# The first head's first keys turned by TensorE, and a normalisation moved ahead of a fold in the last unit

## The chip, the cores and the metric

The kernel runs on one core of one Trainium2 chip. The metric is the device time in microseconds; the time before is the median of three runs. The profile is of one further execution of the same program.

## The reference, cut to what matters

The inputs are a prompt of 2048 tokens of width 512 (A_x), a cache of keys and values for 32 heads of 2048 positions and width 128, and weights. All are bfloat16.

```python
xn = layernorm(x)                                  # 2048 x 512
q = (xn @ wq)  as 32 heads of 128
p = softmax(q @ k_cache^T * 128 ** -0.5)           # 32 x 2048 x 2048
s = (p @ v_cache, heads side by side) @ wo         # 2048 x 512
# B: layernorm, w1, gelu, four shifts by 1 and 2 tokens, w2, residual,
#    layernorm, w3, gelu, w4, residual, on xn
g = silu(B(xn))
out = x + s * g
```

The change touches the attention alone: the keys of head 0 at the start, and the softmax sums and the normalisation of the last heads at the end.

## The kernel before, in words

The program is written in the order in which each engine is to work: `pin` keeps the written order of instructions on each engine and each queue. Pools of SBUF and PSUM buffers decide which later instruction has to wait for an earlier one to be done with a buffer.

**Units and slots.** The attention is cut into 128 units `(g, qt, hh)`: a group of four heads, a tile of 512 queries, and a head of the group. Each unit has 8 slots `p`; slot `n = 8u + p`. In a slot, `s_slot` (L211) makes the scores of two chunks of 128 keys against 512 queries, as `ps_s` with the keys on partitions, and ScalarE takes the exponential into `pT` (L222). Some slots later (`LAGS`, 4 to 12 slots), `pv_slot` (L240) multiplies the same chunk with the values into `ps_o`, of which there are two buffers. Between these matmuls stand the query projections (`q_mm`, L194), the output projection (`wo_mm`, L317) and the matmuls of the other branch (B).

**Keys.** `load_k(h, pieces)` (L168) brings quarters of 512 keys of head `h` from DRAM by a transposing DMA on SyncE's queue, so that `kT` has the 128 head dimensions on partitions. The values come plainly (`load_v`, L177).

**Softmax sums.** VectorE adds the exponentials of a unit (`add_first`, `add_next`, L225 to L233) and halves the sum twice (`fold`, L235, two additions, L237 and L238). For most units (`turned(u)`, units 4 to 125) a DMA turns the result and VectorE reduces it. For the others, `sums` (L251) does it with four matmuls of one column on TensorE, into `ps_sum`. The reciprocal goes to DRAM and comes back to all partitions as `rb` (L263, `bcast` L291). `norm` (L298) multiplies `ps_o` by `rb` into `oT` (L305 for the turned units), which also frees the `ps_o` buffer.

**The start** (L795 to L812). Two token tiles are loaded on SyncE's queue and two on ScalarE's. SyncE then issues the four key quarters of head 0, the values of head 0 and the keys and values of head 1. `warm_up(48)` (L467) has TensorE multiply the identity by itself 48 times. `first_stats` (L418) makes the layer norm of the four tiles on ScalarE, VectorE and GpSimd; ScalarE's last instruction in it is L442, the normalised tile 0. `first_tokens` (L472) has TensorE turn the four tiles (matmul with the identity), copies them back (`back`, L492 on ScalarE and L490 on VectorE), projects the queries in quarters (`q_part`), copies them (`q_back`, L505 and L503), and makes the first scores in halves of 256 queries (`s_half(k, i)`, L507), where `k` is the key quarter. Its written order is turn 0, 1, 3, project 0, turn 2, project 1 and 3, `s_half(0, 0)`, project 2, half of unit 1's query, `s_half(1, 0)`, and so on.

**The last units.** The main loop (L873) writes, for each slot, the scores first, then the values that are due, then the rest. At slot 0 of a unit it writes `add_next(u - 1, 3)` and, where unit `u - 1` is not turned, `fold(u - 1)` (L899 to L902). At slot 1 of units above `LATE` = 20 it writes `normed(u - 3)` (L909). `sums(u - 1)` follows at slot 4 in the last unit (L917). The only unit above `LATE` whose predecessor is not turned is the last, 127.

The functions that the change touches:

Of the kernel before, what the change touches and what calls it, by code (L numbers as in the profile page):

```python
# [8 lines left out]
ACT = mybir.ActivationFunctionType  # L9
ALU = mybir.AluOpType  # L10
FP32 = mybir.dt.float32
BF16 = mybir.dt.bfloat16
# [5 lines left out]
def kernel(  # L18
# [15 lines left out]
    nc = tc.nc  # L34
    P = nc.NUM_PARTITIONS
# [4 lines left out]
    _, H, Sk, Dh = A_k_cache.shape  # L40
# [15 lines left out]
    KSPLIT = 4  # L56
# [4 lines left out]
    WARM = 48  # L61
# [61 lines left out]
    def mm(out, lhsT, rhs, start, stop):  # L123
        mm_count[0] += out.shape[-1] / 512
        pin(nc.tensor.matmul(out=out, lhsT=lhsT, rhs=rhs, start=start, stop=stop))  # L125
# [42 lines left out]
    def load_k(h, pieces):  # L168
        w = Sk // KSPLIT
        for i in pieces:  # L170
            if i == 0:
                kTs[h] = kp.tile([P, Sk], BF16, name="kT")
            pin(nc.sync.dma_start(
                out=kTs[h][:, i * w:(i + 1) * w],
                in_=A_k_cache[0, h, i * w:(i + 1) * w, :], transpose=True))

    def load_v(h, halves, eng=nc.sync):  # L177
        v = A_v_cache[0, h].rearrange("(i p j) d -> p i j d", p=P, j=KJ)
# [56 lines left out]
    def fold(u):  # L235
        a = st[u]["acc"]
        pin(nc.vector.tensor_tensor(out=a[:, 0:2, :], in0=a[:, 0:2, :], in1=a[:, 2:4, :], op=ALU.add))  # L237
        pin(nc.vector.tensor_tensor(out=a[:, 0, :], in0=a[:, 0, :], in1=a[:, 1, :], op=ALU.add))  # L238
# [26 lines left out]
    def turned(u):  # L265
        return T0 <= u < T1
# [148 lines left out]
        pin(nc.vector.bn_aggr(out=mv1[t][:], in_=bn[:]))  # L415
        rsqrt(rs1[t][:], mv1[t][:, 1:2])

    def first_stats():  # L418
        junk = gtp.tile([P, D], BF16, tag="pre", name="pre")
        pin(nc.scalar.activation(  # L420
            out=junk[:], in_=ln[3][:], func=ACT.Identity, scale=1.0 / D, accum_out=mvA[:, 3, 0:1]))
        pin(nc.scalar.activation(
            out=junk[:], in_=ln[3][:], func=ACT.Square, scale=-1.0, bias=mvA[:, 3, 0:1],
            accum_out=mvA[:, 3, 1:2]))
        xn0 = ph1.tile([P, D], BF16, tag="xn", bufs=5, name="xn")
        nb = smp.tile([P, 1], FP32, tag="nm", name="nb")

        def power(t):
            pin(nc.gpsimd.tensor_tensor(
                out=rsA[:, t:t + 1], in0=mvA[:, t, 1:2], in1=nhalf[:, 0:1], op=ALU.pow))  # L430

        for t in range(3):
            pin(nc.vector.bn_stats(out=bnA[:, t, 0:2, :], in_=ln[t][:]))
            pin(nc.vector.bn_aggr(out=mvA[:, t, :], in_=bnA[:, t, :, :]))
            power(t)
            if t == 1:
                pin(nc.vector.tensor_scalar(
                    out=nb[:], in0=mvA[:, 0, 0:1], scalar1=rsA[:, 0:1], scalar2=-1.0, op0=ALU.mult, op1=ALU.mult))
                pin(nc.vector.tensor_scalar(
                    out=mvA[:, 3, 1:2], in0=mvA[:, 3, 1:2], scalar1=1.0 / D, scalar2=EPS, op0=ALU.mult, op1=ALU.add))  # L440
                power(3)
        pin(nc.scalar.activation(  # L442
            out=xn0[:], in_=ln.pop(0)[:], func=ACT.Identity, scale=rsA[:, 0:1], bias=nb[:]))
        xn1 = ln1_norm(1)
        xn3 = ln1_norm(3)
        return xn0, xn1, ln1_norm(2), xn3
# [6 lines left out]
    def ln1_norm(t):  # L453
        xin = ln.pop(t)
        xn = ph1.tile([P, D], BF16, tag="xn", bufs=5, name="xn")
        norm1(t, xn[:], xin[:])
        return xn
# [9 lines left out]
    def warm_up(n):  # L467
        wt = psS.tile([P, 2, 512], FP32, name="ps_s")
        for _ in range(n):
            mm(wt[:, 0, 0:P], ident[:], ident[:], True, True)  # L470
# [327 lines left out]
    pin(nc.scalar.activation(out=act1[:], in_=nhalf[:, 0:1], func=ACT.Identity))  # L798
    for h in range(HG - 1):
        load_w(h, nc.gpsimd)  # L800
    load_k(0, range(KSPLIT))
    load_v(0, (0, 1))
    for i in range(2):
        load_k(1, (2 * i, 2 * i + 1))
        load_v(1, (i,))
    warm_up(WARM)
    xns_0 = first_stats()
    load_w(HG - 1, nc.gpsimd)
    for t in range(4, 6):
        ln1_load(t, nc.gpsimd)  # L810
# [52 lines left out]
    def normed(u):  # L863
        norm(u)
        gg, qq, hh = units[u]
        if hh == HG - 1 and (gg, qq) in deferred:
            at((u + 4) * SPU + 4, lambda: pin(nc.sync.dma_start(out=o_d[(gg, qq)][:], in_=oTs[(gg, qq)][:])))
        elif hh == HG - 1:
            wo_todo.extend((gg, 4 * qq + ts) for ts in range(4))
            if gg == NG - 1:  # L870
                fin_load(4 * qq)

    for n in range(NS):  # L873
        u, p = divmod(n, SPU)
        mm_before = mm_count[0]
        if n >= HALF:
            s_slot(u, p)
        lag = next(v for lim, v in LAGS if n < lim)
        while pv_done <= n - lag:
            pv_slot(*divmod(pv_done, SPU))  # L880
            pv_done += 1
        if n in first_q:
            q_mm(*first_q[n])
        if n == 15:
            q_copy(3)
        if u == HG - 2 and p in (6, 7):
            q_mm(HG, (2 * p - 12, 2 * p - 11))
        if u == HG - 2 and p == 7:
            q_copy(HG)
        if u in (HG - 1, HG):  # L890
            if p < 2:
                q_mm(u + 2, (2 * p, 2 * p + 1))
            if p == 2:
                q_copy(u + 2)
        elif p in (0, 1) and HG < u < NU - 2:
            q_mm(u + 2, (2 * p, 2 * p + 1))
        if p == 0 and u >= 2 and turned(u - 2):
            turned_sums(u - 2)
        if p == 0 and u >= 1:  # L899
            add_next(u - 1, 3)  # L900
            if not turned(u - 1):
                fold(u - 1)  # L902
        if p == (1 if mlp.get("stage") == 2 or u >= QUIET else 2) and HG < u < NU - 2:
            q_copy(u + 2)
        if p == 2 and u >= 1 and turned(u - 1):
            fold(u - 1)
        if p == 3 and u >= 1 and turned(u - 1):
            acc_turn(u - 1)
        if p == 1 and u > LATE:  # L909
            normed(u - 3)  # L910
        if p == (3 if u >= LATE else 2) and u >= 2 and turned(u - 2):
            bcast(u - 2)
        if n in norms:
            normed(norms[n])
        if p == 2 and u > HG + 1 and not turned(u - 2):
            normed(u - 2)
        if p == (4 if u > T1 or u == T0 or u in (1, 2) else 3) and u >= 1 and not turned(u - 1):  # L917
            sums(u - 1)
        if p == (7 if u == 1 else 5 if u > T1 or u in (2, T0) else 4) and u >= 1 and not turned(u - 1):
            bcast(u - 1)  # L920
        if p in (3 if QUIET <= u < NU - 2 else 4, 5) and wo_todo:
            wo_mm(*wo_todo[0], (2, 3) if p == 5 else (0, 1), "xm" if u >= NU - 2 else "xa")
        if p in (1, 3) and u >= NU - 2:
            wo_held(*wo_todo[0], (0, 1) if p == 1 else (2, 3))
        if p == 6 and u >= QUIET:
            add_next(u, 2)
        if p == 6 and wo_box:
            gg, t = wo_todo.popleft()
            wo_post(gg, t)
            if gg == NG - 1:  # L930
                at(n + 5, lambda t=t: wo_out(t))
                if t % 4 < 3:
                    fin_load(t + 1)
        if p == 4:
            add_first(u)
        if p == 6 and u < QUIET:
            add_next(u, 2)
        if p in (2, 6):
            w = 2 * u + (p >= 4)
            want = -(-(w + 1 - W0) * NMM // (W1 - W0)) - done if w >= W0 else 0  # L940
            window = []
            if chunks and want > 0:
                left = chunks[0].size - mpos
                k = min(left, max(2, min(want, 4))) if chunks[0].size > DC else (4 if left == 4 and want >= 3 else 2)
                window = [k - k // 2, k // 2]
        if p in (2, 3, 6, 7) and window:
            for _ in range(window[p % 2]):
                if mpos == 0 and NCH - len(chunks) in hooks:
                    hooks.pop(NCH - len(chunks))(n)
                run = chunks[0]  # L950
                run(mpos, n)
                mpos += 1
                done += 1
                if mpos == run.size:
                    chunks.popleft()
                    mpos = 0
        for fn in todo.pop(n, ()):
            fn()
        x = mm_count[0] - mm_before - 4
        debt[0] = max(0.0, debt[0] + EXP_OVER - x) if n >= HALF else 0.0  # L960
        if act_late and debt[0] + SMALL <= ahead(n + 1) + ahead(n + 2):
            act_late.popleft()(n)
            debt[0] += SMALL
        if p == SPU - 1 and u >= 2 and turned(u - 2) and (u < LATE or u == NU - 1):
            normed(u - 2)
# [95 lines left out]
```

## Time and profile before

| what | before |
|---|---|
| median of three runs | 1247.88 us (1246.97 to 1249.35) |
| profiled execution, its own time | 1246.4 us |
| span of its instructions | 1244.6 us |
| instructions | 16527 |
| granted TensorE clock | 1.00 |
| transposing key loads (`kT`), issues | 128 |

The span runs from the first instruction to the end of the last one. A row of the timeline has start, length, engine, line, operation, output and inputs, count, and in brackets the idle time of the engine ahead of it with what ended it; lengths of several instructions are of the group. PE is the matmul, PEld the weight load of TensorE, and an engine's name with a q is its queue or sequencer. An idle time is put down to what came last by the profile. The chain of waits is followed back from the last instruction.

### The profile page before, as it was taken

Reading aid. Unit: us, or ns where it says so; the run is one execution under the profiler, and the core shown is the slowest. Engines: PE = TensorE matmul, PEld = TensorE weight load, DVE = VectorE, ACT = ScalarE, POOL = GpSimd, SP = SyncE. Lnnn points to the kernel's source line nnn. Section 1 sums busy time; section 2 is a strip of 40 time slices with the busy share of each in tenths; the row PEclk is TensorE's granted clock in tenths of the full one; section 3 lists DMA queues with packets and bytes.
Section 4 is the critical chain, followed back from the end, with each engine's and each line's share of the span. In section 5 each row is a group of like instructions: output and inputs, shape, how many; then the busy total and the mean of one; then the engine's idle time right before and its main releaser. Section 6 shows DMA issues by size and latency. Waiting matters only on the chain.

```text
span 1244.6 us, 16527 instructions
## 1 busy us (share of the span) xinstructions
PE 1232.4 (99%) x5702; PEld 597.3 (48%) x5816; DVE 1116.5 (90%) x1520; ACT 1129.0 (91%) x1285; POOL 172.2 (14%) x299
## 2 busy tenths in 40 slices
PE   9999999999999999999999999999999999999998
PEld 5444444444444444444444444444444444444444
DVE  7999999999899988899988889999888999888998
ACT  8999998888999888899998889998888999998992
POOL 5563003432111000000100000010000000000110
PEclk9999999999999999999999999999999999999999
DMA  9665573665634455234474235734446233563563
GB/s 202 124 118 101 101 141 77 129 126 123 145 65 112 100 102 120 55 89 75 109 148 90 68 77 111 132 76 82 86 101 124 56 89 65 127 140 76 105 149 108
DMA packets 248788, 131.42 MB, mean 106 GB/s; under 512 B 200000, under 2 KB 225472, under 8 KB 248704
## 3 DMA queue, kind: packets, MB, share of 16 engines
q1 hardware_dynamic: 239296, 104.46, 40.8%
q0 software_dynamic: 8832, 25.44, 9.3%
q8 instruction: 45, 0.74, 0.3%
q10 hardware_dynamic: 576, 0.46, 0.1%
q14 instruction: 39, 0.32, 0.1%
HBM read 83.62 MB, written 8.13 MB: 74 GB/s over the span
## 4 chain that ended last, share of the span: by engine, by line
PE 93%; DVE 3%; ACT 1%; DMA 1%; issue 1%; SPq 0%; DVEq 0%; ACTq 0%
PE ps_o L125 34%; PE ps_s L125 33%; PE ps_m L125 9%; PE ps_q L125 8%; PE ps_wo L125 8%; DVE acc L233 1%; ACT pT L222 1%; DMA kT<-in_A_k_cache_dram 1%; DVE oT L305 0%; DVE acc L228 0%; DMA rb<-dr 0%; DVE acc L237 0%; DVE sm L276 0%; DVE sq L554 0%; DVE s_acc L391 0%
## 5 line engine op out<-in xcount | busy, mean ns | idle before, releaser
L222 ACT ACTIVATE pT<-ps_s 128x1024 bf16<-128x1024 f32 x1020 | 1017.7, 1029 | 89.2 <-PE ps_s L125 72.9
L125 PE MATMUL ps_o<-pT,vb 128*128 128x512 bf16 x2027 | 602.9, 379 | 3.8 <-DVE oT L305 0.2
L125 PE MATMUL ps_s<-qT,kT 128*128 128x512 bf16 (+1 forms) x1992 | 595.3, 378 | 2.2 <-DMA kT<-in_A_k_cache_dram 0.7
L125 PEld LDWEIGHTS <-kT 128*128 128x128 bf16 x2056 | 232.4, 113 | 227.2 <-issue 2.4
L233 DVE TENSOR_TENSOR acc<-acc,pT 128x2048 bf16<-128x2048 bf16 x256 | 310.5, 1213 | 15.6 <-ACT pT L222 14.7
L125 PEld LDWEIGHTS <-vb 128*128 128x128 bf16 x2048 | 200.2, 98 | 225.8 <-issue 0.5
L228 DVE TENSOR_TENSOR acc<-pT 128x2048 bf16<-128x2048 bf16 x128 | 156.2, 1220 | 32.2 <-ACT pT L222 31.8
L125 PE MATMUL ps_q<-xnT,wq_h 128*128 128x512 bf16 (+1 forms) x517 | 151.3, 374 | 0.5
L125 PE MATMUL ps_wo<-wo_h,oT 128*128 128x512 bf16 (+1 forms) x453 | 133.8, 377 | 0.2
L305 DVE TENSOR_TENSOR oT<-ps_o,rb 128x512 bf16<-128x512 f32 x122 | 130.8, 1072 | 2.1 <-DMA rb<-dr 2.0
L391 DVE TENSOR_TENSOR s_acc<-ps_wo,s_acc 128x512 f32<-128x512 f32 x96 | 66.0, 687 | 41.2 <-PE ps_wo L125 40.5
L237 DVE TENSOR_TENSOR acc<-acc 128x1024 bf16<-128x1024 bf16 x128 | 87.4, 683 | 0.3
L276 DVE TENSOR_REDUCE sm<-accT 128x4 f32<-128x512 bf16 x122 | 82.8, 678 | 1.5 <-DMA accT<-acc 1.4
L125 PEld LDWEIGHTS <-wq_h 128*128 128x128 bf16 x524 | 50.7, 98 | 59.5 <-issue 0.8
L208 DVE CAST qT<-ps_q 128x512 bf16<-128x512 f32 x109 | 75.0, 688 | 3.1 <-PE ps_q L125 2.8
L125 PE MATMUL ps_m<-xn2T,w_sb 128*128 128x512 bf16 x218 | 75.3, 379 | 0.1
L125 PE MATMUL ps_m<-w_sb,h2T 128*128 128x512 bf16 x218 | 75.3, 379 | 0.1
L723 POOL DMA_DIRECT2D w_sb<-in_B_w_dram x28 | 21.1, 755 | 370.2 <-PE ps_m L125 328.4
L125 PEld LDWEIGHTS <-oT 128*128 128x128 bf16 x468 | 45.7, 98 | 54.5 <-DVE oT L312 0.5
L751 POOL DMA_DIRECT2D g_d<-xr x16 | 8.8, 548 | 438.3 <-DVE xr L749 438.3
L238 DVE TENSOR_TENSOR acc<-acc 128x512 bf16<-128x512 bf16 x128 | 54.4, 425 | 4.4
L554 DVE SCALAR_TENSOR_TENSOR sq<-sq,pre 128x1024 bf16<-128x1024 bf16 x36 | 44.0, 1222 | 4.6 <-ACT sq L550 4.5
(102 smaller groups left out, 633.5 us busy)
## 6 DMA issues: line engine op xcount, KB each, us to landing
rb<-dr SPq DMA_DIRECT2D x127, 256.0 KB, 3.8
vb<-in_A_v_cache_dram SPq DMA_DIRECT2D x62, 256.0 KB, 3.8
w_sb<-in_B_w_dram POOLq DMA_DIRECT2D x28, 256.0 KB, 4.6
wo_h<-in_A_wo_dram SPq DMA_DIRECT2D x32, 128.0 KB, 3.8
wq_h<-in_A_wq_dram SPq DMA_DIRECT2D x28, 128.0 KB, 3.5
kT<-in_A_k_cache_dram SPq DMA_TRANSPOSE x128, 3.8
dr<-rc SPq DMA_DIRECT2D x128, 2.0 KB, 2.4
xr<-in_A_x_dram POOLq DMA_DIRECT2D x16, 128.0 KB, 3.3
```

The source lines that it names most:

```text
L125: pin(nc.tensor.matmul(out=out, lhsT=lhsT, rhs=rhs, start=start, stop=stop))
L208: pin(nc.vector.tensor_copy(out=qT[:], in_=st[u].pop("psq")[:]))
L222: pin(nc.scalar.activation(out=s["pT"][-1][:, jj:jj + 2, :], in_=sps[:], func=ACT.Exp, scale=SCALE))
L228: pin(nc.vector.tensor_tensor(out=s["acc"][:], in0=s["pT"][0][:], in1=s["pT"][1][:], op=ALU.add))
L233: pin(nc.vector.tensor_tensor(out=a[:], in0=a[:], in1=st[u]["pT"][i][:], op=ALU.add))
L237: pin(nc.vector.tensor_tensor(out=a[:, 0:2, :], in0=a[:, 0:2, :], in1=a[:, 2:4, :], op=ALU.add))
L238: pin(nc.vector.tensor_tensor(out=a[:, 0, :], in0=a[:, 0, :], in1=a[:, 1, :], op=ALU.add))
L276: pin(nc.vector.tensor_reduce(out=sm[:], in_=s.pop("at")[:], axis=mybir.AxisListType.X, op=ALU.add))
L305: pin(nc.vector.tensor_tensor(out=oTs[(g, qt)][:, hh, :].rearrange(f, j=4), in0=s["o"].rearrange(f, j=4), in1=s["rb"].rearrange("x (p j) - ...
L391: pin(nc.vector.tensor_tensor(out=sa, in0=ps[:], in1=sa, op=ALU.add))
L554: pin(nc.vector.scalar_tensor_tensor(out=sq[:].rearrange(f2), in0=sq[:].rearrange(f2), scalar=1.0, in1=pre[:].rearrange(f2), op0=ALU.add, ...
L723: pin(nc.gpsimd.dma_start(out=w[:], in_=w3_v[:, :, fc * P:(fc + 2) * P]))
```

## The change

The first quarter of head 0's keys is no longer brought by a transposing DMA. `first_keys` loads it plainly, on the same queue and at the same place, into a tile `kn` with four consecutive keys on each partition (1 KB). `first_keys_turn` turns it on TensorE with four matmuls against the identity, into a PSUM buffer of the tag `xm`, in the place of four of the warm-up matmuls; four more warm-up matmuls follow it, so that there are 40, 4 and 4 where there were 48. `first_keys_back` copies it on ScalarE into the first quarter of `kT`, in the order that the transposing DMA gave, behind L442. `kn` takes a buffer of the tag `pre` ahead of the other users of that tag. The other three quarters of head 0, and all other heads, are loaded as before.

In the last unit, `fold(u - 1)` moves from slot 0 to slot 1, behind `normed(u - 3)`.

```diff
     def load_k(h, pieces):
         w = Sk // KSPLIT
         for i in pieces:
-            if i == 0:
+            if h not in kTs:
                 kTs[h] = kp.tile([P, Sk], BF16, name="kT")
...
+    def first_keys():
+        kTs[0] = kp.tile([P, Sk], BF16, name="kT")
+        kn = gtp.tile([P, KJ, Dh], BF16, tag="pre", name="kn")
+        pin(nc.sync.dma_start(
+            out=kn[:], in_=A_k_cache[0, 0, 0:Sk // KSPLIT, :].rearrange("(p j) d -> p j d", j=KJ)))
+        return kn
+
+    def first_keys_turn(kn):
+        tp = psX.tile([P, KJ, P], FP32, tag="xm", name="ps_k")
+        for j in range(KJ):
+            mm(tp[:, j, :], kn[:, j, :], ident[:], True, True)
+        return tp
+
+    def first_keys_back(tp):
+        pin(nc.scalar.activation(
+            out=kTs[0][:, 0:Sk // KSPLIT].rearrange("d (p j) -> d j p", j=KJ), in_=tp[:], func=ACT.Identity))
...
-    def first_stats():
+    def first_stats(behind):
...
             out=xn0[:], in_=ln.pop(0)[:], func=ACT.Identity, scale=rsA[:, 0:1], bias=nb[:]))
+        behind()
         xn1 = ln1_norm(1)
...
-    load_k(0, range(KSPLIT))
+    kn_0 = first_keys()
+    load_k(0, range(1, KSPLIT))
     load_v(0, (0, 1))
...
-    warm_up(WARM)
-    xns_0 = first_stats()
+    warm_up(WARM - 8)
+    tp_0 = first_keys_turn(kn_0)
+    warm_up(4)
+    xns_0 = first_stats(lambda: first_keys_back(tp_0))
...
             add_next(u - 1, 3)
-            if not turned(u - 1):
+            if not turned(u - 1) and u <= LATE:
                 fold(u - 1)
...
         if p == 1 and u > LATE:
             normed(u - 3)
+            if not turned(u - 1):
+                fold(u - 1)
```

## The prediction

> **What bounds the kernel now.** I read the page first, then TensorE's waits over the whole run, then the chain of waits, and then the timeline at the two places that the change touches.
>
> ```profile
> span 1244.6 us, 16527 instructions
> PE 1232.4 (99%) x5702; PEld 597.3 (48%) x5816; DVE 1116.5 (90%) x1520; ACT 1129.0 (91%) x1285; POOL 172.2 (14%) x299
> PE 93%; DVE 3%; ACT 1%; DMA 1%; issue 1%; SPq 0%; DVEq 0%; ACTq 0%
> ```
>
> TensorE (PE) is busy for 99% of the span, and 93% of the chain that ends last is its work. A gain can only come from time in which TensorE stands. The waits of TensorE in the whole run are three groups:
>
> ```profile
> PE ps_s L125 <- DVE ident L87: 1.4, 1, 1.4
> PE ps_s L125 <- DMA kT<-in_A_k_cache_dram: 0.7, 2, 0.5
> PE ps_o L125 <- DVE oT L305: 0.2, 1, 0.2
> ```
>
> The first is the start before the identity exists, and the change leaves it. The second is two waits for the first head's keys, the third one wait for a normalisation. The change goes at exactly these two. The chain at the start, in order of time (start, length, what):
>
> ```profile
> 1.65 1.23 SPq L173
> 2.92 7.28 DMA kT<-in_A_k_cache_dram
> 10.25 0.63 PE ps_s L125 x4
> 10.88 0.43 PE ps_q L125 x2
> ```
>
> So the run hangs on the second quarter of the keys: its transposing DMA is issued behind the first one on SyncE's queue, lands 7.28 us later at 10.20, and TensorE goes on at 10.25. From there TensorE has no recorded wait until the last normalisation at 1217: what the stream gains before 10.25 is kept to the end unless a new wait eats it.
>
> **Part 1, the first keys.** The rows of the start (start, length, engine, line, operation, count):
>
> ```profile
> 0.73 0.87 SPq L408 DMA_DIRECT2D xin<-in_A_x_dram  x2
> 1.39 4.74 PE L125 MATMUL ps_s<-ident 128*128 128x128 bf16 x48 [1.39 <-DVE ident L87]
> 1.65 5.13 SPq L173 DMA_TRANSPOSE kT<-in_A_k_cache_dram  x4
> 5.18 0.81 ACT L442 ACTIVATE xn<-xin,nb,rsA 128x512 bf16<-128x512 bf16 x1
> 6.48 1.08 ACT L492 ACTIVATE xnT<-ps_o 128x512 bf16<-128x512 f32 x2 [0.49 <-PE ps_o L125]
> 8.04 0.38 ACT L505 ACTIVATE qT<-ps_q 128x256 bf16<-128x256 f32 x1
> 9.01 0.63 PE L125 MATMUL ps_s<-qT,kT 128*128 128x256 bf16 x4 [0.52 <-DMA kT<-in_A_k_cache_dram]
> 9.47 0.60 PE L125 MATMUL ps_q<-xnT,wq_h 128*128 128x128 bf16 x5
> 10.25 0.63 PE L125 MATMUL ps_s<-qT,kT 128*128 128x256 bf16 x4 [0.18 <-DMA kT<-in_A_k_cache_dram]
> ```
>
> And the DMAs issued in the first 15 us (median us from issue to landing is last):
>
> ```profile
> vb<-in_A_v_cache_dram SPq DMA_DIRECT2D x4, 256.0 KB, 5.3
> wq_h<-in_A_wq_dram POOLq DMA_DIRECT2D x4, 128.0 KB, 5.7
> xin<-in_A_x_dram SPq DMA_DIRECT2D x2, 128.0 KB, 2.7
> kT<-in_A_k_cache_dram SPq DMA_TRANSPOSE x9, 6.4
> ```
>
> *SyncE's queue.* One of four transposing issues (5.13 / 4 = 1.28 us) becomes a plain one of the same 128 KB (0.87 / 2 = 0.44). Whatever stands behind it on SyncE is issued 0.84 us sooner: the second quarter of the keys at 2.10 in place of 2.92, then the third and fourth, the values and the next head's keys.
>
> *The plain keys, kn.* Issued at 1.65 behind the two x loads. The nearest row is that of those loads (same size, form and queue): 2.7 us, so 4.35. Bounds: not below 2.7, since it queues behind them; above, the value loads' 5.3 (6.95) and, at worst, the landing of the transposing load whose place it takes (8.95, just ahead of the matmul at 9.01 that waits for it). I take 4.5 to 5.0.
>
> *TensorE.* Forty of the 48 warm-up matmuls stay ahead of the turn. By the row's mean (4.74 / 48 = 0.1 us) the turn would stand at 5.3, an estimate that I give 0.3 us either way. Four matmuls that turn the keys and four that warm take the place of the last eight of the same form: no work is added, and nothing waits if kn has landed by about 5.3. If it has not, the token turns queued behind it wait too, and with them ScalarE.
>
> *ScalarE.* One new 128x512 copy out of PSUM stands between L442 (ends 5.99) and the first L492 (6.48). Two L492 in a row take 1.08, so 0.54 each; the hole is 0.49, which L492 spent waiting for TensorE. Cost on the path: 0.05 us. Its output is written with a stride of four elements, which no row of this kernel's ScalarE shows; bounds: nothing (a copy of that size out of PSUM is 0.54) and a doubling (another 0.54). I take nothing, because the L492 rows already read and write in pieces and cost no more than their size.
>
> *First scores.* They wait at 9.01 for kT. Without it they wait for the query copy L505, which ends at 8.42 and then, with 0.05 for the new copy and 0.05 for the signal, they start at 8.52: 0.49 sooner. The work between the first and the second score group (four matmuls of 256 columns, four of 128, two of 512) takes 10.25 - 9.01 - 0.18 = 1.06 by its rows, less if a record of the 9.47 group is missing, then up to 1.12. So the second group can start at 8.52 + 1.1 = 9.62, if its keys are there.
>
> *Second quarter of the keys.* It now has the place that the first had: issued at 2.10 in place of 1.65. The first landed 8.95 - 1.65 = 7.3 us after issue; the same gives 9.4, before 9.62. Bounds: 8.95 if landing is set by the other transfers and not by the issue, and 10.2 as now if it gains nothing. **Front: 10.25 - 9.62 = 0.63 us gained**, between 0.05 (landing at 10.2) and 0.7.
>
> [...]
>
> **Part 2, the normalisation.** It changes one unit, the last: two fold additions and one normalisation swap places on VectorE. Rows of VectorE and TensorE there:
>
> ```profile
> 1207.10 1.07 DVE L305 TENSOR_TENSOR oT<-ps_o,rb 128x512 bf16<-128x512 f32 x1
> 1208.09 0.68 DVE L237 TENSOR_TENSOR acc<-acc 128x1024 bf16<-128x1024 bf16 x1
> 1208.81 0.42 DVE L238 TENSOR_TENSOR acc<-acc 128x512 bf16<-128x512 bf16 x1
> 1215.31 0.69 DVE L237 TENSOR_TENSOR acc<-acc 128x1024 bf16<-128x1024 bf16 x1
> 1216.04 0.43 DVE L238 TENSOR_TENSOR acc<-acc 128x512 bf16<-128x512 bf16 x1
> 1216.38 1.07 DVE L305 TENSOR_TENSOR oT<-ps_o,rb 128x512 bf16<-128x512 f32 x1
> 1216.70 0.59 PE L125 MATMUL ps_s<-qT,kT 128*128 128x512 bf16 x2
> 1217.50 0.59 PE L125 MATMUL ps_o<-pT,vb 128*128 128x512 bf16 x2 [0.21 <-DVE oT L305]
> 1217.93 0.27 PE L125 MATMUL ps_sum<-ones_t,acc 128*128 128x1 bf16 x4
> 1225.37 0.21 PEld L125 LDWEIGHTS <-acc 128*128 128x128 bf16 x4 [0.30 <-DVE acc L238]
> ```
>
> The two score matmuls at 1216.70 would be followed 0.43 us later, as pairs are (10.88 in the chain), at 1217.13; the value matmuls start at 1217.50, when the normalisation has freed their PSUM buffer: 0.37 lost. In the new order it starts at 1215.31, where the fold did, and ends at 1216.38, before the value matmuls want the buffer at 1217.13; that wait goes. Its row from DRAM is needed 1.07 us sooner:
>
> ```profile
> L295 SPq DMA_DIRECT2D rb<-dr x2: 327/387/447, 1210.6 to 1217.5; - x2
> DMA to landing us min/median/max: 3.5/3.5/3.5
> ```
>
> Issued at 1210.6, landed at 1214.1: there in time. What is late next is the fold, which the sums read. From the triple at 1207.10, normalisation and both folds take 1208.81 + 0.42 - 1207.10 = 2.13, so the folds end at 1217.44, the sums want them at 1217.93 - 0.37 = 1217.56, with a weight load just ahead; the one at 1225.37 started 0.06 after its fold, so here 1217.50. Queued behind on TensorE is everything else, so a late fold costs one for one: I take 0.07, bounds 0 and 0.2. **Tail: 0.30 us gained**, between 0.17 and 0.37. VectorE's work behind the pair starts when it did (same three durations), and after 1217.5 the end follows TensorE.
>
> **Sum.** 0.63 + 0.30 = 0.93 us off the profiled execution: 1246.4 becomes 1245.5 (span 1244.6 to 1243.7). The profiled execution lies 1.5 under the median of the three runs, 1247.88, and those reach from 1246.97 to 1249.35. Off the median: **1247.0 us**, 0.07% faster. About 0.2% (2.5 us) is what a measurement of this kernel can tell from no change, so this is a forecast of no difference that shows.
>
> **Rivals.**
>
> *The second quarter lands no sooner* (about 10.2). For it: its landing lies among those of wq_h (5.7 us) and may be set by them. Against: it then has one transposing load fewer ahead. Front 0.05, total -0.35: 1247.5.
>
> *The tokens of the second query tile eat the gain.* Their last transposing load and the first matmul that reads it:
>
> ```profile
> L465 SPq DMA_TRANSPOSE xnT<-xn x1: 1283/1283/1283, 26.8 to 26.8; - x1
> DMA to landing us min/median/max: 3.8/3.8/3.8
> ...
> 30.66 0.59 PE L125 MATMUL ps_q<-xnT,wq_h 128*128 128x512 bf16 x2
> ```
>
> 26.8 + 3.8 = 30.6, and TensorE reads it at 30.66: no slack at all. If TensorE comes 0.63 sooner and this load does not, 0.6 is given back: total -0.3, 1247.6. Against it: SyncE's queue, on which it stands, is 0.84 sooner at the start.
>
> *Slower: kn lands late.* The turn stands in TensorE's order ahead of every token turn. kn must land by about 5.4 (four matmuls, then the copy of 0.54, before 6.48). Later it delays the first scores one for one; the front's gain is gone at 6.0, the tail's at 6.35. At the value loads' 5.3 us (6.95) the total is +0.6: 1248.5. At 8.95 it is +2.6: 1250.5. For it: most loads around it take 5 to 6 us. Against: the two ahead of it in its queue take 2.7.
>
> *The swap does nothing* (fold and sums late by as much as the normalisation is early): total -0.6, 1247.3.
>
> **How the numbers follow.** Forecast 0.60; second quarter no sooner 0.13; tokens 0.12; kn late 0.08; swap without effect 0.07. All but the extreme of the slow rival stay within 2.5 us of the present time. What reaches over the bound is mostly the spread of the runs (2.4 us between three of them): from -0.9 it takes 1.6 more to be faster by over 0.2%, chance 0.09, and 3.4 to be slower, which with the extreme of kn gives 0.05; within 0.2% 0.86. The range takes the same gain off the profiled execution and the highest run: 1246.4 - 0.9 = 1245.5 and 1249.35 - 0.9 = 1248.5, which holds all cases but the extreme one.
>
> **What would show it.** TensorE's waits for kT from DMA gone or under 0.1, and none for kn; first scores near 8.5, second near 9.6; SyncE's third entry 0.44 long; the first token matmul still near 6.05; the matmul at 30.66 near 30.0 without a wait; the value matmuls of the last unit 0.43 behind the scores. A first token matmul after 6.3 shows kn late; a second score group after 10.0 shows the second quarter unmoved; a wait of the sums for L238 over 0.2 us shows the swap empty. A time outside 1245.5 to 1248.5 with none of these waits in the trace would come from a mechanism that I have not named.

## The result, and the profile after

| | before | after |
|---|---|---|
| median (lowest to highest), 14 runs each | 1247.10 us (1246.58 to 1249.35) | 1249.74 us (1246.80 to 1252.02) |
| profiled execution, its span | 1246.4, 1244.6 us | 1248.48, 1246.7 us |

The ratio after to before is 1.0017 (95% interval 1.0010 to 1.0024): the change costs 2.6 us between the medians and 2.1 by the ratio. The ratio on record is not the quotient of the two medians, here as in the table below. A later measurement of the same two kernels, on one chip, gave 1.0015 (1.0006 to 1.0024), 1248.07 against 1246.49. The forecast was 0.9 us less, range 1245.5 to 1248.5; the time is above the range. The runs of after also spread over 5.2 us, those of before over 2.8; in the later measurement they spread over 2.8 and 3.0.

TensorE's waits in the whole run of after (engine, tile, line, releaser; us in total, times, longest):

```profile
PE ps_s L125 <- DVE ident L87: 1.4, 1, 1.4
PE ps_k L125 <- DMA kn<-in_A_k_cache_dram: 1.3, 1, 1.3
PE ps_q L125 <- issue: 0.5, 1, 0.5
PE ps_s L125 <- ACT qT L523: 0.2, 1, 0.2
```

The waits that the change aimed at, two for kT and one for the normalisation, are gone. A wait for kn stands in their place, and one without a named releaser. The chain of waits at the start of after (start, length, what):

```profile
1.65 5.44 DMA kn<-in_A_k_cache_dram
7.13 0.62 PE ps_k L125 x4
7.78 1.31 ACT kT L191
9.09 0.43 ACT xnT L510
...
11.18 0.60 PE ps_s L125 x4
11.78 0.44 PE ps_q L125 x5
...
12.27 0.60 PE ps_s L125 x4
```

Before, the run hung on the second quarter of the keys up to 10.25. Now it hangs on the new plain load, then on the new copy. The second score group starts at 12.27 in place of 10.25, **2.02 us later**. The timeline of after at that place:

```profile
1.39 4.45 PE L125 MATMUL ps_s<-ident 128*128 128x128 bf16 x40 [1.39 <-DVE ident L87]
1.65 0.42 SPq L180 DMA_DIRECT2D kn<-in_A_k_cache_dram  x1
2.12 3.81 SPq L173 DMA_TRANSPOSE kT<-in_A_k_cache_dram  x3
...
7.13 0.61 PE L125 MATMUL ps_k<-ident,kn 128*128 128x128 bf16 x4 [1.30 <-DMA kn<-in_A_k_cache_dram]
7.54 0.63 PE L125 MATMUL ps_s<-ident 128*128 128x128 bf16 x4
...
7.96 1.06 PE L125 MATMUL ps_o<-ident,xn 128*128 128x128 bf16 x8
```

The forty warm-up matmuls end at 5.84, and TensorE, whose order is pinned, stands 1.30 us, to 7.13, for kn, which lands at 7.09; the first token matmul goes from 6.05 to 7.96. The next place is the second query tile. The last two transposing loads of its tokens in after, and TensorE's row that reads the last one:

```profile
L483 SPq DMA_TRANSPOSE xnT<-xn x2: 1201/1209/1217, 25.7 to 27.0; - x2
DMA to landing us min/median/max: 5.2/5.7/6.2
```

```profile
32.19 0.59 PE L125 MATMUL ps_o<-pT,vb 128*128 128x512 bf16 x2
33.31 0.59 PE L125 MATMUL ps_q<-xnT,wq_h 128*128 128x512 bf16 x2 [0.53 <-issue]
```

The load issued at 27.0 takes 6.2 us (3.8 before) and lands at 33.2. The matmul behind it starts 1.12 after its neighbour in place of 0.43: **0.69 us lost**. And the last unit, from the timeline of after:

```profile
1217.45 1.07 DVE L322 TENSOR_TENSOR oT<-ps_o,rb 128x512 bf16<-128x512 f32 x1
1218.44 0.68 DVE L254 TENSOR_TENSOR acc<-acc 128x1024 bf16<-128x1024 bf16 x1
1219.15 0.42 DVE L255 TENSOR_TENSOR acc<-acc 128x512 bf16<-128x512 bf16 x1
1219.17 0.59 PE L125 MATMUL ps_s<-qT,kT 128*128 128x512 bf16 x2
1219.60 0.59 PE L125 MATMUL ps_o<-pT,vb 128*128 128x512 bf16 x2
1220.04 0.28 PE L125 MATMUL ps_sum<-ones_t,acc 128*128 128x1 bf16 x4
```

The normalisation stands ahead of both folds; the value matmuls follow the scores by 0.43 where it was 0.80, and the sums at 1220.04 find the fold done at 1219.57: **0.37 us gained**. Together +2.02 + 0.69 - 0.37 = +2.34; the spans differ by 2.1. The last unit's scores come 2.47 later than before (1219.17 against 1216.70), so the missing 0.24 was made up between the second tile and the last unit; where is not shown.

### The profile page after: what moved, and what is told of

Same layout as the page of the kernel before. It is cut to its first block, busy times and chain, and to the rows that moved or that the text cites. A ratio compares the mean times of both kernels' runs of the same rounds, so it can differ in the third digit from the quotient of the medians.

```text
span 1246.7 us, 16529 instructions
## 1 busy us (share of the span) xinstructions
PE 1233.3 (99%) x5702; PEld 598.9 (48%) x5816; DVE 1116.0 (90%) x1520; ACT 1130.1 (91%) x1286; POOL 173.1 (14%) x299
## 4 chain that ended last, share of the span: by engine, by line
PE 97%; ACT 1%; DVE 1%; issue 1%; DMA 0%; SPq 0%; ACTq 0%
PE ps_o L125 36%; PE ps_s L125 35%; PE ps_m L125 10%; PE ps_q L125 9%; PE ps_wo L125 8%; ACT pT L239 1%; DMA kn<-in_A_k_cache_dram 0%; DVE acc L250 0%; ACT kT L191 0%; DVE sq L572 0%; DVE oT L322 0%; SPq L425 0%; ACT pre L609 0%; PE ps_sum L125 0%; PE ps_k L125 0%
```

## The experiments

Four questions: is the tail's gain real; why does kn land late; what do the wait and the copy each cost; why do the second tile's tokens come late. Kernels in neighbouring rows with the same time of before ran on one chip and share those runs. A letter for a theory belongs to its own expectation; the words beside it count. "kn" below is the time from its issue (at 1.65 unless the edit moves it) to its landing.

| run | median us (runs) | before, same chip | ratio, 95% interval | kn, us |
|---|---|---|---|---|
| e1 swap only | 1246.42 (11) | 1246.97 | 0.9997, 0.9988 to 1.0005 | none |
| e2 keys only | 1248.69 (11) | 1246.97 | 1.0013, 1.0004 to 1.0022 | 5.1 |
| e3 dense copy | 1247.09 (11) | 1246.97 | 1.0001, 0.9992 to 1.0010 | 4.6 |
| e4 turns behind | 1247.46 (11) | 1246.97 | 1.0005, 0.9996 to 1.0013 | 4.6 |
| e5 wq behind | 1252.76 (1) | 1246.77 | none | 3.4 |
| e6 two wq behind | 1250.45 (6) | 1246.77 | 1.0031, 1.0019 to 1.0042 | 4.1 |
| e7 tokens behind | 1247.85 (11) | 1246.77 | 1.0007, 0.9998 to 1.0016 | 6.2 |
| e8 both | 1249.64 (9) | 1246.77 | 1.0024, 1.0014 to 1.0033 | 4.2 |
| e9 wq after norm | 1248.34 (11) | 1247.12 | 1.0009, 1.0000 to 1.0018 | 4.2 |
| e10 swap, tokens | 1246.76 (11) | 1247.12 | 0.9998, 0.9990 to 1.0007 | none |
| e11 late turn, tokens | 1246.88 (11) | 1247.12 | 0.9999, 0.9990 to 1.0008 | 5.1 |
| e12 late turn, wq | 1248.91 (11) | 1247.12 | 1.0018, 1.0009 to 1.0027 | 4.2 |
| e13 late turn | 1247.10 (11) | 1246.49 | 1.0006, 0.9997 to 1.0015 | 6.2 |
| e14 after again | 1248.07 (11) | 1246.49 | 1.0015, 1.0006 to 1.0024 | 4.9 |
| e15 dense again | 1248.10 (11) | 1246.49 | 1.0008, 0.9999 to 1.0017 | 5.1 |

### The two parts alone: e1 and e2

e1 is before with the last unit's fold behind the normalisation; e2 is before with the keys' part alone.

```diff
-            if not turned(u - 1):
+            if not turned(u - 1) and u <= LATE:
...
             normed(u - 3)
+            if not turned(u - 1):
+                fold(u - 1)
```

> Part 2 alone: the keys are loaded as before, only the normalisation stands in front of the fold in the last unit. Theory (the swap takes away the last wait of TensorE, 0.37 us, and brings none): 0.3 to 0.4 us below before, and the value matmuls of the last unit 0.43 us behind the scores. Rival (the fold is now late for the sums): no gain, and a wait of the sums for L238.

> Part 1 alone, the order of the last unit as before. Theory (the whole loss is at the start): 2.4 to 3 us above before, kn landing near 7 us, the second score group near 12.3. Rival (part of the loss comes from the swap): less than 2 us above before.

The swap alone: TensorE's rows in the last unit of e1.

```profile
1216.43 0.59 PE L125 MATMUL ps_s<-qT,kT 128*128 128x512 bf16 x2
1216.86 0.59 PE L125 MATMUL ps_o<-pT,vb 128*128 128x512 bf16 x2
1217.30 0.27 PE L125 MATMUL ps_sum<-ones_t,acc 128*128 128x1 bf16 x4
```

Scores, values and sums follow at 0.43: the 0.37 is there without the keys' part. The median is 0.55 lower, which the interval (0.9988 to 1.0005) can't tell from nothing.

The start of e1 is that of before. Still, the only wait of TensorE in its whole run is this one:

```profile
PE ps_s L125 <- DVE ident L87: 1.4, 1, 1.4
```

There is no wait for kT: the first two key quarters landed at 7.31 and 9.30, and the scores started at 9.14 and 10.23. e10, the third profile with this start, has no such wait either (landed at 5.34 and 7.98, scores at 8.90 and 9.99). From issue to landing the first quarter took 7.3 us in before, 5.7 in e1 and 3.7 in e10. **The 0.7 us of waits for kT that the keys' part aimed at stand in one of three profiles of the old start.**

The keys' part alone carries the whole loss: 1.7 us, interval above 1. That is below the 2.4 to 3 of the theory and within the rival's "less than 2", but the rival's cause, a loss from the swap, is not what e1 shows. In e2 TensorE waits 1.1 us for kn and 0.9 more for ScalarE's token copy, which stands behind the key copy.

### Why kn is late: e4, e5, e6, e8

e4 issues the values ahead of the three transposing key loads, so that no transposing load follows kn directly. e5 lets all three first wq_h loads on GpSimd wait for kn (a one-column copy of kn on GpSimd is the wait); e6 and e8 let the second and third wait.

The edit of e4:

```diff
     kn_0 = first_keys()
-    load_k(0, range(1, KSPLIT))
     load_v(0, (0, 1))
+    load_k(0, range(1, KSPLIT))
```

The edit of e5; in e6 and e8, which also have the dense copy of e3 (e8 the token loads of e7 too), the first load_w stays ahead of the copy:

```diff
+    kn_0 = first_keys()
+    pin(nc.gpsimd.tensor_copy(out=diag[:, 0:1], in_=kn_0[:, 0, 0:1]))
     for h in range(HG - 1):
         load_w(h, nc.gpsimd)
-    kn_0 = first_keys()
```

> The whole change, but SyncE issues the two halves of head 0's values ahead of the three transposing key loads. Theory A (kn's completion is held up because the transposing loads and the wq_h loads run on the DMA engines together): kn lands at 4.5 to 5.3 us and the time is 1 to 2 us below the changed kernel. Theory B (the wq_h loads alone hold it up): kn still lands near 7. Theory C (the transposing loads behind it in the same queue alone hold it up): kn lands at 4.5 to 5.3, as under A; the run that holds back wq_h tells A from C.

> The changed kernel, but GpSimd issues its three wq_h loads only when kn has landed. One look at kn's landing; the time is not the question, since the query projection then waits for wq_h. Theory B (the wq_h loads hold up kn's completion): kn lands at 4.3 to 5.0 us. Rival (what stands around it is not the cause, the third load of a queue is late anyway, or the transposing loads behind it do it): kn still lands at 6 or later.

> The changed kernel with the dense copy, and the second and third wq_h load (not the first) issued only when kn has landed. Theory B: kn lands at 4.5 to 5.5 in place of 6.3 to 7.1, the first token matmul stands at 6.1 to 6.3, and TensorE's first scores come 0.5 to 1 us sooner than with the dense copy alone; the time falls by as much only if the token loads do not take it back. Rival: kn lands after 6, no gain.

> The changed kernel with the dense copy and both moves: two wq_h loads behind kn, and the five token loads behind the transposing ones. If both theories hold, the front is 0.5 to 0.7 us ahead of before, no wait stands at the second query tile, and the time is 0.7 to 1.2 us below before. If the second quarter of the keys or the wq_h loads become late instead, no gain over before.

The landing of kn in e5 (issue duration; then issue to landing), and TensorE's largest wait there:

```profile
L180 SPq DMA_DIRECT2D kn<-in_A_k_cache_dram x1: 424/424/424, 1.6 to 1.6; - x1
DMA to landing us min/median/max: 3.4/3.4/3.4
```

```profile
PE ps_o L125 <- ACT xn L459: 3.7, 1, 3.7
```

With the wq_h loads held, kn lands 3.4 us after issue, at 5.00, the upper end of what the forecast had assumed. With one of them beside it (e6, e8, e9, e12) it takes 4.1 to 4.2, with three (e2 to e4, e7, e11, e13 to e15, and after) 4.6 to 6.2. The second quarter of the keys follows: 3.9 to 4.1 us when they are held, 5.5 to 7.5 when not. Nine profiles stand against five, without overlap, and the order is the same on each of the two chips that had both kinds (6.2 in e7 against 4.1 and 4.2 in e6 and e8; 5.1 in e11 against 4.2 in e9 and e12). The 3.4 is a single profile. How late a load comes beside the three wq_h is chance in part: the transposing quarter of the old start took 3.7 to 7.3 beside them.

In e4 kn lands at 6.23, between what A (4.5 to 5.3) and B (near 7) had. It takes 4.6, the low end of the range with three wq_h. The transposing loads were not moved out of its way: the first is issued at 3.11 in place of 2.12, and the values stand ahead of it. So the delay came with the wq_h loads, and the transposing loads with no wq_h beside them did not make it (3.4 in e5); whether they add to it is not shown.

The times of e5, e6 and e8 are worse for a reason of the edit: the waiting copy and the wq_h issues stand on GpSimd ahead of the power operations of the first layer norm, and xn comes 3.2 to 3.7 us late. These three runs tell of the landing, not of the price.

### The wq_h loads behind the norm: e9 and e12

The same hold without that side effect: the second and third wq_h loads are issued behind the norm's power operations. e9 has this on top of e7 (below), e12 on top of e11.

```diff
-    for h in range(HG - 1):
-        load_w(h, nc.gpsimd)
+    load_w(0, nc.gpsimd)
...
-    load_w(HG - 1, nc.gpsimd)
+    for h in range(1, HG):
+        load_w(h, nc.gpsimd)
```

> After with the dense key copy and with token loads 8 to 12 on SyncE, and now the second and third wq_h loads are issued on GpSimd behind the four power operations of the first layer norm, so that they neither run beside the first quarter of the keys nor stand ahead of the norm. Theory A (the wq_h loads beside it make kn late): kn lands at 5.0 to 5.8, TensorE waits 0.5 us or less for it, no long wait of ps_o for xn, first scores at 8.5 to 8.9, and with the tail's 0.37 about 1246.2 us in the median, 0.7 below before. Rival (kn is late for another reason and the edits that waited for kn only hid it): kn at 6.2 or later, a wait of 1.0 or more, first scores at 9.2 or later, 1247.1 or above. A new wait of the second head's query projection for its wq_h load (issued near 5.3, needed near 10) would show at ps_q.

> The late turn of the run before it together with the second and third wq_h loads behind the layer norm's power operations. If the wq_h loads hold back both kn and the second quarter of the keys, kn lands by 5.8, the second quarter by 8.5, first scores at 8.5, second group at 9.6, and the median is 1246.0 to 1246.3, the front gain that was forecast for the change. If only the order on TensorE mattered, it equals the late turn alone within 0.2; if the later wq_h loads are themselves missed, the wait shows at ps_q and the median is above it.

e9: the landings of kn and of the second quarter are early, and the wait moves to the weights.

```profile
L180 SPq DMA_DIRECT2D kn<-in_A_k_cache_dram x1: 424/424/424, 1.6 to 1.6; - x1
DMA to landing us min/median/max: 4.2/4.2/4.2
```

```profile
PE ps_q L125 <- DMA wq_h<-in_A_wq_dram: 1.8, 2, 1.5
```

kn lands at 5.8, there is no recorded wait for it, and the first scores start at 9.36; then the second and third heads' projections wait 1.8 us for the weights that were held (3.3 in e12, whose profile is of its longest run, 1251.24). The landings are as expected. The first scores of e9 (8.5 to 8.9 expected) and the times are not: 1248.34 and 1248.91 where about 1246.2 was expected. The third case of e12's expectation, that the held weights are themselves missed, is what came. **The loads that delay the keys are themselves wanted at about 10 us; whichever goes first, the other is late** (kn 4.6 to 6.2 us after its issue, or the weights with waits of 1.8 and 3.3).

### The copy and the clock: e3, e15, e14

e3 and e15 are the same kernel: the changed one with the key copy written densely and read with the stride. e14 is the changed kernel itself.

```diff
-            out=kTs[0][:, 0:Sk // KSPLIT].rearrange("d (p j) -> d j p", j=KJ), in_=tp[:], func=ACT.Identity))
+            out=kTs[0][:, 0:Sk // KSPLIT].rearrange("d (p j) -> d p j", j=KJ),
+            in_=tp[:].rearrange("d j p -> d p j"), func=ACT.Identity))
```

> The whole change, but ScalarE's copy of the turned keys writes them densely and reads PSUM with a stride instead. Theory (the 1.31 us of that copy, against 0.59 for the same size elsewhere, is its strided write): the copy takes about 0.6 us, the first scores come 0.7 us sooner after kn than in the changed kernel, and the time is 0.7 us below the changed kernel. Rival (a stride on the reading side, or what runs beside it, costs the same): the copy still takes 1.2 us or more.

> The changed kernel itself, unaltered, on the same chip as its two neighbours, as the yardstick for them: 1249 to 1250 us, 0.1 to 0.2% above before, with a wait for kn of 1.0 to 2.1 us. If it stands within 0.5 of before here, the loss belongs to chance in the landings and not to the kernel.

> The changed kernel with the dense key copy alone, as run once already, now beside the changed kernel on one chip. If the copy's 0.71 us stands on the path one for one, its median is 0.5 to 1.0 below that of the changed kernel; if the difference of 2.6 us seen across chips was the copy's doing, 2 or more below.

The copy in e3's timeline, then TensorE's rows of the turn, of the eight matmuls of the first two tokens and of the first scores, in e3 and in e15:

```profile
6.75 0.60 ACT L191 ACTIVATE kT<-ps_k 128x512 bf16<-128x512 f32 x1 [0.68 <-PE ps_k L125]
```

```profile
6.32 0.40 PE L125 MATMUL ps_k<-ident,kn 128*128 128x128 bf16 x4 [1.00 <-DMA kn<-in_A_k_cache_dram]
6.55 0.39 PE L125 MATMUL ps_s<-ident 128*128 128x128 bf16 x4
6.78 0.61 PE L125 MATMUL ps_o<-ident,xn 128*128 128x128 bf16 x8
...
9.24 0.60 PE L125 MATMUL ps_s<-qT,kT 128*128 128x256 bf16 x4
```

```profile
6.79 0.61 PE L125 MATMUL ps_k<-ident,kn 128*128 128x128 bf16 x4 [0.96 <-DMA kn<-in_A_k_cache_dram]
7.19 0.63 PE L125 MATMUL ps_s<-ident 128*128 128x128 bf16 x4
7.62 1.06 PE L125 MATMUL ps_o<-ident,xn 128*128 128x128 bf16 x8
...
10.82 0.60 PE L125 MATMUL ps_s<-qT,kT 128*128 128x256 bf16 x4 [0.25 <-ACT qT L524]
```

Written densely the copy takes 0.60 in place of 1.31: the stride of four elements in the output is what it cost. But look at the groups of four matmuls of 128 columns. In e3 they start 0.23 apart (6.55 to 6.78), in e15 0.43 (7.19 to 7.62): **TensorE at half rate in e15, at full rate in e3, in the same program**; the two rates are these two spacings. In after it is 0.42 (7.54 to 7.96). The forty warm-up matmuls show it as well: 4.45 us in after, e14 and e15, which had not come to full rate when the wait began, 3.93 in e3 and 3.81 in e4, which had. So e15's kn came 0.47 later and its first scores 1.58 later. From the turn to the first scores, by copy and rate, out of the same two rows of each timeline:

| | full rate | half rate |
|---|---|---|
| dense copy | 2.92 (e3), 2.91 (e7) | 4.03 (e15) |
| strided copy | 3.57 (e4) | 4.34 (e14), 4.05 (after) |

e2, strided, changed its rate on the way (4.13) and is left out. The copy's stride costs 0.65 at full rate and 0 to 0.3 at half rate, where TensorE's own rate is what the tokens wait for (in e15 it has no recorded wait from 6.79 up to the 0.25 ahead of 10.82); the half rate costs 0.5 to 1.1. In the medians the copy is not seen: 1248.10 dense, 1248.07 strided, against an expected 0.5 to 1.0 apart. By the ratios (1.0008 and 1.0015) the dense kernel is 0.9 lower, and the intervals overlap; what the copy costs the whole run is not settled. e14 itself came 1 us below the 1249 to 1250 expected, with a wait for kn of 0.7, and still 1.6 above before: the loss is not the chance of one measurement.

Of seven profiles with the turn inside the warm-up and a wait for kn (e6, with its later wait for xn, left out), four (after, e2, e14, e15) ran such matmuls at half rate after 8.9; of six with 48 unbroken warm-up matmuls (before, e1, e10 to e13) none did. The unbroken ones came to full rate at 5.1 to 7.3; after, e14 and e15 not before 10.1; e3, e4 and e7 were there by 4.4 to 7.9, before or during the wait. The granted clock column reads 1.00 in this stretch of after all the same; only the lengths of the matmuls show it.

Why the rate rises early in one execution and late in another was not shown. e3 and e15 are the same program, one at full rate before the wait for kn, one not until 10.2. The spread of the runs does not show it either: 5.2 us for after's first fourteen, but 2.8 for the eleven of e14, where before's runs on the five occasions spread over 2.6 to 4.4.

### The second tile's tokens: e7 and e10

The transposing token loads of the second query tile run beside plain token loads from GpSimd's queue for later tiles. e7 (on e3) and e10 (on e1) issue loads 8 to 12 on SyncE instead, behind the last transposing load.

```diff
-            at({11: 24, 12: 25}.get(t, max(stats - 8, 2)), lambda t=t: ln1_load(t, nc.gpsimd))
+            if 8 <= t <= 12:
+                at(16 + (t - 8) // 2, lambda t=t: ln1_load(t, nc.sync))
+            else:
+                at(max(stats - 8, 2), lambda t=t: ln1_load(t, nc.gpsimd))
```

> The changed kernel with the dense copy, and the five token loads that GpSimd issues around 24 to 27 us (tiles 8 to 12) put on SyncE's queue behind the transposing load of the last tile of the second query tile. Theory D (that transposing load lands late because these plain loads run beside it): it lands within 4.5 us of its issue, TensorE's wait at the second query tile's first projection falls from 2.0 us to under 0.3, and the time is 1 to 2 us below the dense copy alone. Rival (the transposing load is late because of the keys ahead of it in its own queue): it still takes 6 us or more and the wait stays.

> Before with the swap of the last unit alone and token loads 8 to 12 on SyncE; the start is that of before. If the tail's 0.37 is a real gain and the tokens cost nothing in before's order (0.04 us of slack), the median is 1246.5 to 1246.7, 0.4 below before, and the wait for kT at the second score group stays. If moving token loads brings a new wait of its own (a later xin on SyncE's queue), it is 1247.0 or more.

The last two transposing loads of the second tile in e3, which has the plain loads beside them, and TensorE's row behind them:

```profile
L484 SPq DMA_TRANSPOSE xnT<-xn x2: 1202/1210/1217, 23.8 to 25.1; - x2
DMA to landing us min/median/max: 6.5/7.1/7.7
```

```profile
32.84 0.59 PE L125 MATMUL ps_q<-xnT,wq_h 128*128 128x512 bf16 x2 [2.01 <-DVE acc L251]
```

(The trace names acc, but acc feeds no such projection; the load issued at 25.1 lands at 32.8.) The last three in e7:

```profile
L484 SPq DMA_TRANSPOSE xnT<-xn x3: 1207/1210/1213, 23.0 to 26.7; - x3
DMA to landing us min/median/max: 2.4/2.4/2.6
```

With the plain loads behind them they take 2.4 to 2.6 in place of 6.5 to 7.7, and the wait is gone. In the six profiles with the five loads moved (e7 to e12) the last two take 2.4 to 3.0, in the eleven others 3.8 to 7.7: it was the plain loads beside them. It does not pay: in e10 the moved loads stand ahead of two value loads on SyncE's queue, and a value matmul waits 1.57 us at 39.20; the trace names xn for the matmul, but vb for its weight load (2.05), and vb at the same place in e11 (0.39). e10 stands at 0.9998, e1 without the move at 0.9997. In e7's own profile kn took 6.2 us and TensorE waited 2.1 for it, which hid the gain.

### The turn in another place: e11 and e13

The turn of kn moved behind the third token turn and the first quarter of the query projection, 48 warm-up matmuls again, its copy dense and on VectorE. e13 is this on e3's tokens, e11 on e7's.

```diff
-    warm_up(WARM - 8)
-    tp_0 = first_keys_turn(kn_0)
-    warm_up(4)
-    xns_0 = first_stats(lambda: first_keys_back(tp_0))
+    warm_up(WARM)
+    xns_0 = first_stats()
...
         q_part(0)
+        first_keys_back(first_keys_turn(kn))
```

> After with token loads 8 to 12 on SyncE, and the turn of kn moved in TensorE's order from the warm-up to behind the third token turn and the first quarter of the query projection (near 8.0 us), its copy dense and on VectorE ahead of the copy of the fourth token tile. Theory (the loss at the front is TensorE standing for a load that lands at 6 to 8 us while the token turns queue behind it): no wait for kn up to a landing of 7.5, first token matmul back at 6.05, first scores at 8.5 to 9.0, second group by 10.0, median 1246.2 to 1246.6. If instead the front is set by the landing of the second quarter or by the token chain, the second group stays at 10.2 or later and the median is 1246.9 or more.

> After with the dense key copy on VectorE and the turn of kn behind the third token turn; the token loads stay where after has them. If the place of the turn on TensorE is the main cost, the median is 1.5 to 2.5 us below that of after on the same chip and within 0.5 of before, and TensorE has no wait for kn. What is left would then be the wait of the second query tile for its tokens (0.5 to 2 us). If the place matters little and the copy's length does (1.31 against 0.60), it equals the dense copy in after's place within 0.3.

TensorE's rows in e11:

```profile
6.12 0.78 PE L125 MATMUL ps_o<-ident,xn 128*128 128x128 bf16 x8
...
7.43 0.39 PE L125 MATMUL ps_k<-ident,kn 128*128 128x128 bf16 x4
...
8.83 0.60 PE L125 MATMUL ps_s<-qT,kT 128*128 128x256 bf16 x4
...
9.92 0.60 PE L125 MATMUL ps_s<-qT,kT 128*128 128x256 bf16 x4
```

kn lands at 6.7, no earlier than in other runs, and nothing waits for it. The scores start at 8.83 and 9.92, 0.18 and 0.33 sooner than before: part of the front gain that was forecast, and the tokens at 6.12 are where they were. Its median of 1246.88 misses the 1246.2 to 1246.6 expected. On one chip e13 stands 1.0 us below the changed kernel by the medians (1247.10 against 1248.07) and the dense copy in the old place 0.03 above it; the expected 1.5 to 2.5 is missed. Read so, the turn's place counts and not the copy's length. But by the ratios e13 (1.0006) and the dense copy in the old place (1.0008) stand side by side below the changed kernel (1.0015), which is the rival's sign, and all three intervals overlap. Which of the two carries the gain is not settled. In e13's profile, that of its longest run, the first wq_h landed late as well (a wait of 0.6), the scores started at 9.96 and 11.05, later than before, and the second tile's tokens cost 0.7.

No version beats before by more than its interval; e1, e10 and e11 stand within 0.03% of it.

## Why the prediction was wrong, point by point

- **The landing of kn** is the step that failed: "I take 4.5 to 5.0", measured 7.09 in after, 6.2 to 7.9 in all profiles without a hold. It was sized by the row of the same form and queue, the x loads (2.7), but those are issued from 0.73 on, ahead of the three wq_h loads (1.35 on) and the transposing ones. The rows of what is in flight at the same time, which stood in the same list (wq_h 5.7, vb 5.3, kT 6.4), were the nearer ones. e5 shows the assumed 5.0 when the wq_h loads are held. The bounds (2.7 after issue, so 4.35, to 8.95) contained it, and the rival "kn lands late" named the mechanism, the place and the queue behind it; its 0.08 was far too low, and the range stopped at its mildest form.
- **Its price.** The rival had one for one from 5.4, less the front gain: at 7.09 the second scores would be 1.09 later than before. They are 2.02 later. The missing 0.9 is the copy (0.77 over its term) and the half rate; the two overlap, as the table of four cases shows, and are not added. In the whole span, 1246.7 against the 1243.7 forecast, kn by its own price is 1.7 of the 3.0 that were missed, copy and rate 0.9, the second tile 0.7, less 0.3 that the tail and a place not named gave back.
- **What there was to gain.** The 0.63 at the front was read from one profile. e1 and e10 have the same start and no wait for kT, so part of it was the chance of that execution; and e11, with nothing waiting for kn, had 0.33 of it.
- **The warm-up's end**, forecast at 5.3, is 5.84 in after. The mean of 0.1 us over 48 matmuls mixed the slow first ones with the fast last ones (in before a single one took 0.31 us up to 5.1 and 0.22 from 5.4 on); at half rate all forty take 4.45 / 40 = 0.11 each. In e3 (1.39 + 3.93 = 5.32) and e4 (5.20) the forecast came out: it depends on when the full rate comes.
- **The key copy**: 0.54 taken, doubling as the bound; 1.31, above the bound. That the L492 rows "read and write in pieces" was no evidence for a stride of four elements: their pieces are 128 elements in a row.
- **The second quarter of the keys**: forecast 9.4, landed 2.1 + 6.6 = 8.7, sooner than the bound of 8.95. Right in direction; TensorE was not there yet to use it. The 2.7 us (x loads) and the 7.3 (the first quarter) by which the two landings were sized differ by the moment more than by the kind of load: in e5 the plain kn took 3.4 and the transposing quarter issued next 4.0.
- **SyncE's queue**: the third entry 0.42 long and the second quarter issued at 2.12, as forecast.
- **The second tile's tokens**: the rival (no slack at 30.66) was right about the place. The cause given, TensorE coming sooner, was not: TensorE came later and waited 0.69, since the load itself took 6.2 in place of 3.8 beside GpSimd's loads.
- **The tail**: 0.30 forecast, 0.37 in the profile of after, and the same rows in e1. The folds cost TensorE nothing, the lower bound of that term.
- **The spread.** The range carried over that of before's three runs. The changed start has a chance of its own in it, the landing of kn and the rate of TensorE behind it, but a wider spread (5.2 against 2.8) was not seen again in e14 (2.8 against 3.0). The 0.2% taken for the least difference that shows was too coarse: the interval is 0.07% to either side, and a loss of 0.17% shows.

## What to carry to other kernels

Size a new load by the rows of what is in flight at the moment of its issue, not by the row of its own form at a quieter moment; then ask which of the others comes late in exchange. Work that waits for such a load belongs as far back in the pinned order of its engine as its reader allows, and not inside a warm-up: with the turn in it four of seven profiles ran matmuls of 128 columns at half rate after 8.9, with 48 unbroken matmuls none of six. e13, 1.0 us below the changed kernel by the medians, points that way without showing it. Before a change is spent on a wait, look for that wait in a second and a third execution: here it was missing from two of three. A strided output of a copy is to be priced by a row that has this stride, or bounded beyond a doubling.

## What the hardware showed that was not expected

- A plain 128 KB load on SyncE's queue took 3.4 us with no wq_h load on GpSimd's queue beside it (one profile), 4.1 to 4.2 with one and 4.6 to 6.2 with three. The last two transposing token loads took 3.8 to 7.7 us beside five plain loads from GpSimd's queue and 2.4 to 3.0 without them. A transposing key load issued at 1.65 in the same start took 7.3, 5.7 and 3.7 us in three profiles.
- A ScalarE copy of 128x512 from PSUM took 0.60 us with a dense bfloat16 output and 1.31 with a stride of four elements; a strided read from PSUM cost about nothing (0.60 too for the single token copy at 7.46 in before).
- When TensorE comes to full rate changes from one execution to the next (48 warm-up matmuls took 4.74 us in before and 5.30 in e1, the same start), and in e2 it fell back. The rows of its stream there, behind the wait of 1.06 us and around the one of 0.93:

```profile
7.66 0.39 PE L125 MATMUL ps_s<-ident,xn 128*128 128x128 bf16 x4
8.98 0.58 PE L125 MATMUL ps_q<-xnT,wq_h 128*128 128x128 bf16 x4 [0.93 <-ACT xnT L510]
9.36 0.63 PE L125 MATMUL ps_s<-ident,xn 128*128 128x128 bf16 x4
9.78 1.06 PE L125 MATMUL ps_q<-xnT,wq_h 128*128 128x128 bf16 x8
10.89 1.01 PE L125 MATMUL ps_s<-qT,kT 128*128 128x256 bf16 x4
```

The group of four at 7.66 is at full rate (0.39), those from 8.98 on are not (0.58 to 0.63). It is the one fall behind waits as short as these: e4 stayed at full rate through 1.08 and 0.93 (0.38 at 8.49), after, e14 and e15 had not risen yet, and e7 was at full rate (0.40 at 7.90) behind a wait of 2.06. In e6, with a wait of 3.21 between them, a group of four took 0.39 at 6.03 and 0.63 at 10.46; in e12, behind a wait of 2.1 that ends at 15.09, pairs of 512 columns went from 0.45 at 16.14 to 0.85 at 16.59, and the granted clock from 15 to 20 reads 0.66. What makes the rate fall was not shown.
